# Attention value sums held in one PSUM bank for sixteen units

## The chip, the cores and the metric

One Trainium2 chip, one core of it. The metric is the device time of one execution, in microseconds, as the median of three runs. The engines are TensorE (PE, with its weight loads, PEld), VectorE (DVE), ScalarE (ACT), GpSimd (POOL) and SyncE (SP), which issues the transfers.

## The reference

Two mixers of 2048 rows of 512 are computed and blended by a gate. Branch A is a Fourier transform over the hidden and the sequence axis, as products with cosine and sine matrices; branch B is attention with 32 heads of 16.

```python
a = jnp.einsum("bsd,ed->bse", x, dft_hid_re)
b = jnp.einsum("bsd,ed->bse", x, dft_hid_im)
y = jnp.einsum("ts,bse->bte", dft_seq_re, a) - jnp.einsum("ts,bse->bte", dft_seq_im, b)
...
scores = jnp.einsum("bhqd,bhkd->bhqk", q, k) * scale
p = _softmax(scores, axis=-1)
o = jnp.einsum("bhqk,bhkd->bhqd", p, v)
...
g = _sigmoid((x * gate_w).sum(-1, keepdims=True))
return g * a + (1 - g) * b
```

## The kernel before

All products run on TensorE. The heads are worked in 16 pairs. For each pair the scores are made twice: once as tiles of 128 queries by 512 keys, of which VectorE takes the row maxima (line 260), and once transposed, 128 keys by 512 queries with the maximum already subtracted in the product, of which ScalarE takes the exponential into the SBUF tile `pt` (line 798). A **unit** `u` is one block of 128 keys against 1024 queries of one half `hf`, for both heads of the pair: four exponential tiles, two blocks of 512 queries (`qb`) for each of two heads (`h`). Sixteen units make one half of a pair; there are 512 units.

The **value sum** of a unit is four matmuls of 32 columns each (line 833), one for each query block and head, that fill one PSUM bank together. `pv(us)` takes two units into a bank (`start` on the first, `stop` on the second); then ScalarE copies the bank into `oe` (line 842), and GpSimd adds `oe` onto the SBUF tile `osum` (line 848). For the first two units of a half ScalarE copies straight into `osum` (line 839). After the sixteenth unit SP stores `osum` to memory (line 851). The last sixteen units go through `pv_last`, which holds a bank for eight units and is another code path.

The order of the work is written out by hand as patterns (lines 940 to 943), one **run** to a pattern. Each letter is a slot: `a` a tile for a maximum (line 258), `s` a score tile for an exponential (line 797), and beside a slot stands one matmul `d` of the Fourier chain or of the output projection (line 473). Those use 64 rows of the array each, so a slot's tile and its `d` run side by side on the two halves of the array. The bar at the end of a pattern calls `values()`, which takes the sum of two units.

```python
    FULL = "a s a s a s a s s a s a s a a s |"
    THIN = "aS s a s a s s a s a s a a sA |"
    EVEN = "aA s s a s ^ s d s sA a d sS |", "a s a sS a ^ s a s s s s a |"
    TEN = "aA s s a s ^ s s s a a sS |", "a s a sS a ^ s s s s s aA |"
```

`pairs()` issues 24 runs of THIN, 192 of FULL and 32 of EVEN and TEN; eight more runs of the last sixteen units end the kernel.

PSUM has eight banks here. One (`psD`) is kept for the Fourier chain, seven circulate: `bank()` hands out the one that the planner's estimate `free[]` says comes back first, and `read_by` estimates when its reader is done. What is handed out is fixed when the program is built; on the chip a matmul into a bank waits for the semaphore of the reader before. `pt` has four buffers.

Of the kernel before, what the change touches and what calls it, by code (L numbers as in the profile page):

```python
# [10 lines left out]
F32 = mybir.dt.float32  # L11
F32R = mybir.dt.float32r
AF = mybir.ActivationFunctionType
ALU = mybir.AluOpType
AX = mybir.AxisListType

P = 128
S = 2048
D = 512
H = 32  # L20
DH = 16
NP = H // 2
KT = D // P
NT = S // P
UNITS = NP * 32
# [7 lines left out]
def mix_kernel(ctx: ExitStack, tc: tile.TileContext, xa_t, xa, wqkv, w_hid, w_seq, wo, gate_w, out):  # L33
# [5 lines left out]
    nc = tc.nc  # L39
# [11 lines left out]
    o_d = [dram.tile([NP, 64, S // 2], F32, name=f"o{hf}") for hf in range(2)]  # L51
# [27 lines left out]
    def turn_of(kind):  # L79

        group = {"f": banks, "s": banks[:4], "a": [*banks[4:], psD], "r": [banks[6], banks[4]]}[kind]
        turns[kind] += 1
        pool = group[(turns[kind] - 1) % len(group)]
        return pool.tile([P, 512], F32, name="d" if pool is psD else "t")
# [47 lines left out]
    with tc.tile_pool(name="qk", bufs=1, reuse_waits="tile") as pool:  # L132
# [27 lines left out]
        ps = turn_of("f")  # L160
# [3 lines left out]
        x, raw = xab[0][:, :, :, :P], first[0].rearrange("p (s t) -> p s t", s=4)  # L164
        nc.scalar.copy(x[:, :, 0], raw)
        for ct in range(4):
            cols = slice(ct * P, (ct + 1) * P)
# [14 lines left out]
        for tb in range(4):  # L182
# [4 lines left out]
            for c in range(2):  # L187
                if tb == 0 and c == 0:
                    pss = [turn_of("f") for _ in range(4)]
                    for kt, w, v in [(kt, w, v) for kt in range(2) for w, v in ((wh, 0), (wl, 0), (wh, 1))]:  # L190
                        for ct in range(4):
                            nc.tensor.matmul(pss[ct], w[:, c, kt, ct * P:(ct + 1) * P],  # L192
                                             xab[tb][:, :, v, kt * P:(kt + 1) * P],
                                             start=kt == 0 and w is wh and not v, stop=False)
# [7 lines left out]
                for ct in range(4):  # L202
                    ps = turn_of("f")
# [13 lines left out]
    vt = main.tile([P, NT, NP, 33], F32, name="vt")  # L217
# [156 lines left out]
    for s in range(4):  # L374
        ps = turn_of("s")
# [21 lines left out]
    work = ctx.enter_context(tc.tile_pool(name="work", bufs=1, side="right", reuse_waits="tile"))  # L397
# [28 lines left out]
    now, free, dve, act = 0.0, [0.0] * 7, 0.0, 0.0  # L426

    def bank(i=None):

        nonlocal now  # L430
        if i is None:
            i = min(range(7), key=lambda j: free[j])
        now = max(now, free[i] + 0.7)
        return i, banks[i].tile([P, 512], F32, name="t")

    def read_by(i, kind):

        nonlocal dve, act
        if kind == "a":
            dve = max(now + 2.0, dve) + 2.6  # L440
            free[i] = dve + 0.4
        else:
            act = max(now + 2.0, act) + 2.1
            free[i] = act + 0.5
# [209 lines left out]
    few, by_others = [], set()  # L654

    def finish(ps, t, y, other=False, n=1):
        if other:

            for c in range(n):
                cols = slice(c * D // n, (c + 1) * D // n)  # L660
                tmp = few[0][:, t % 4, cols]
                nc.scalar.activation(tmp, ps[:, cols], AF.Copy, scale=omg[:, t:t + 1])
                nc.gpsimd.tensor_tensor(y[:, cols], y[:, cols], tmp, ALU.add)
            return
        nc.vector.scalar_tensor_tensor(y, ps, omg[:, t:t + 1], y, op0=ALU.mult, op1=ALU.add)  # L665
# [100 lines left out]
    last_pairs = []  # L766

    def last_pair(fill):
        few.append(work.tile([P, 4, D], F32, name="few", tag="pt", bufs=4))
        x = last_pairs[1]  # L770
        x.copy(4)
        by_others.add(6)
        pump(fill, 3)
        x.turn()
        pump(fill, 3)
        x.back()
        drain(fill)
        x.products((0,))


    pts = {}

    def scores(u, qb, h, ps=None):
        p, r = divmod(u, 32)
        hf, kt = divmod(r, 16)
        q0 = hf * 1024 + qb * 512
        if u >= UNITS - 16:

            blk, kt = divmod(kt, 8)
            q0, kt = 1024 + blk * 512, 2 * kt + qb  # L790
        if u not in pts:
            pts[u] = work.tile([P, 4, 512], F32, name="pt", bufs=4)
        if ps is None:
            i, ps = bank()
            read_by(i, "s")
        rr = slice(64 * h, 64 * h + 64)
        nc.tensor.matmul(ps, ks[p % 2][rr, kt * P:(kt + 1) * P], qs[p % 2][rr, q0:q0 + 512], start=True, stop=True)  # L797
        return nc.scalar.activation(pts[u][:, 2 * qb + h], ps, AF.Exp, bias=0.0, scale=DH ** -0.5)  # L798

    held = []  # L800

    def pv_last(u):
        nonlocal now
        blk, k2 = divmod(u - UNITS + 16, 8)
        pt = pts.pop(u)
        if k2 == 0:
            i, acc = bank()
            free[i] = 1e9
            held[:] = [i]
            last_pairs.append(LastPair(blk, acc))  # L810
        acc = last_pairs[-1].acc
        for j in range(4):
            x, h = divmod(j, 2)
            nc.tensor.matmul(acc[32 * j:32 * j + 32], vt[:, 2 * k2 + x, NP - 1, h:h + 32], pt[:, j],  # L814
                             start=k2 == 0, stop=k2 == 7)
        now += 3.75
        if blk == 0 and k2 == 7:
            last_pairs[0].copy(1)
            free[held[0]] = now + 6

    osum = work.tile([P, 2, 512], F32, name="osum", tag="w15")

    def pv(us):

        nonlocal now
        i, acc = bank()
        for u in us:
            p, r = divmod(u, 32)
            hf, kt = divmod(r, 16)
            pt = pts.pop(u)  # L830
            for j in range(4):
                h = j % 2
                nc.tensor.matmul(acc[32 * j:32 * j + 32], vt[:, kt, p, h:h + 32], pt[:, j],  # L833
                                 start=u == us[0], stop=u == us[-1])
        now += 3.75 * len(us) + 1
        read_by(i, "s")
        o = osum[:, hf]
        if kt + 1 == len(us):
            nc.scalar.copy(o, acc)
            return  # L840
        oe = work.tile([P, 512], F32, name="oe", bufs=2)
        nc.scalar.copy(oe, acc)  # L842
        adds.append(partial(add_sum, o, oe, p, hf, kt == NT - 1))

    adds = []

    def add_sum(o, oe, p, hf, whole):
        nc.gpsimd.tensor_tensor(o, o, oe, ALU.add)  # L848
        if whole:
            for qb in range(2):  # L850
                nc.sync.dma_start(o_d[hf][p, :, qb * 512:(qb + 1) * 512], o[64 * qb:64 * qb + 64])

    def add_sums():
        while adds:
            adds.pop(0)()

    def take(gen, n, whole=True):

# [23 lines left out]
    def pump(gen, n):  # L882
        for x in take(gen, n, False):
            issue(x, None)
# [11 lines left out]
    for p in range(2, NP):  # L896
        u = 32 * (p - 1)
        at(u - 18, load_q, p, LOW)
        for kb in range(4):
            cols = slice(kb * 512, (kb + 1) * 512)  # L900
# [7 lines left out]
    for hf in range(2):  # L908
        for ct in range(4):
            n = 3 if hf and ct == 3 else 4  # L910
# [43 lines left out]
    users, valued = [], 0  # L954
# [8 lines left out]
            else:  # L963
                users.append((kind, scores(*x)))

    def values():
        nonlocal valued
        us = valued, valued + 1
        valued += 2
        if us[0] < UNITS - 16:  # L970
            pv(us)
        else:
            for u in us:
                pv_last(u)

    def segment(pattern, half, ds, stop, between=None, hold=True):


        nonlocal now
        nonlocal users  # L980
        before, users = users, []
        ds, late = iter(ds), []
        back = late if hold else None
        for n, slot in enumerate(pattern.split()):
            if slot == "|":
                for f in late:
                    f()
                add_sums()
                run_plan(valued)
                if between:  # L990
                    between()
                values()
                continue
            if slot == "^":
                if deferred:
                    deferred.pop(0)()
                continue
            now += 1
            ahead = n and len(slot) == 1 and slot != "d" and pattern in (THIN, *TEN)
            if ahead:  # L1000
                score(slot[0], 1 - half)
            if len(slot) == 1:
                x = next(ds, None)
                if x:

                    before = before if x[0].begun else None
                    i = issue(x, half, stop, back)
                    users = []
                    if before:
                        tc.add_manual_dep(  # L1010
                            i.ins, dict(before[::-1]).get("s", before[0][1]).ins.name,
                            mybir.DependencyInfo(mybir.DependencyClass.Sync, mybir.DependencyReason.DATA))
                        before = None
            if not ahead and slot != "d":
                score(slot[0], 1 - half)
            if len(slot) == 2:
                score(slot[1].lower(), half)
        if deferred:
            deferred.pop(0)()
# [46 lines left out]
    for hf, qts in ((1, range(2)), (1, range(2, 5)), (1, range(5, 8)), (0, range(2))):  # L1066
        for half in range(2):
            ds = take(proj(hf, (3,), [held_bank] * (len(qts) - 1) + one, qts, half == 1), 9, False)
            pattern = "s s ^ s s s s s s |" if len(qts) < 3 else "s s ^ s s d s s s s |"
            if valued == UNITS - 2:  # L1070
                pattern = "s s s s d d |"
# [39 lines left out]
```

## Time and profile before

| | |
|---|---|
| median of three runs | 1651.18 us (1650.62 to 1653.74) |
| span of the profiled execution | 1649.2 us |
| TensorE busy, matmuls | 1641.4 us |
| VectorE busy | 1356.8 us |
| ScalarE busy | 1268.2 us |
| GpSimd busy | 754.5 us |
| copies into `oe` (line 842) | 217, 588 ns each, 127.5 us |
| additions onto `osum` (line 848) | 217, 1289 ns each, 279.7 us |

The profile is of one execution; its span of 1649.2 us lies 2.0 us below the median. Matmul records of TensorE are pipelined and their ends modelled, so its busy share does not tell how close it is to its best; the steps from one matmul to the next do. A row of a group has line, engine, operation, output and inputs, sizes and count, then busy time and the mean length of one in ns, and last the idle time of the engine before it and what ended it. Each value matmul of the program is two records in the trace.

### The profile page before, as it was taken

What the parts mean: (1) busy time and instruction counts of PE and PEld (TensorE: products, weight loads), DVE (VectorE), ACT (ScalarE), POOL (GpSimd) and SP (SyncE); (2) the same over time, 40 slices, a digit from 0 to 9 for tenths busy, and PEclk for the clock granted to TensorE, in tenths of its full rate; (3) what the DMA queues carried; (4) which work ended last, traced back from release to release, by engine and by line L of the source; (5) the groups of instructions that cost most, each with busy time, mean ns of one, the idle gap of its engine ahead of it and who ended that gap; (6) DMA issues with size and microseconds to landing.
All of it is one profiled execution on the core that took longest, in us unless ns stands there. A gap on an engine that the chain in (4) does not pass through costs nothing.

```text
span 1649.2 us, 35245 instructions
## 1 busy us (share of the span) xinstructions
PE 1641.4 (100%) x13169; PEld 1017.0 (62%) x13169; DVE 1356.8 (82%) x2285; ACT 1268.2 (77%) x2487; POOL 754.5 (46%) x813
## 2 busy tenths in 40 slices
PE   9999999999999999999999999999999999999998
PEld 7888855556656666566665666666666556655544
DVE  5469988888888888888888888888888888877776
ACT  5312188888888888888888888887888888899996
POOL 0224643554544555545454565554545566332341
PEclk9999999999999999999999999999999999999999
DMA  9953301112221224222227334322222233451024
GB/s 291 353 161 135 155 14 38 29 53 66 67 72 52 62 86 134 74 62 70 57 75 258 86 94 116 96 77 68 66 72 74 81 111 107 156 195 45 15 53 143
DMA packets 93346, 165.67 MB, mean 100 GB/s; under 512 B 23456, under 2 KB 26408, under 8 KB 92024
## 3 DMA queue, kind: packets, MB, share of 16 engines
q1 hardware_dynamic: 88536, 162.64, 31.9%
q8 instruction: 104, 1.70, 0.4%
q0 software_dynamic: 4352, 0.39, 0.2%
q14 instruction: 66, 0.54, 0.1%
q10 hardware_dynamic: 288, 0.39, 0.1%
HBM read 107.73 MB, written 54.52 MB: 98 GB/s over the span
## 4 chain that ended last, share of the span: by engine, by line
PE 99%; DMA 0%; DVE 0%; ACT 0%; DVEq 0%; SPq 0%; issue 0%
PE d L473 46%; PE t L833 28%; PE t L258 6%; PE t L797 6%; PE t L354 5%; PE t L92 2%; PE t L91 2%; PE t L93 2%; PE t L814 1%; PE t L473 1%; PE t L378 1%; PE t L192 0%; DMA raw<-wqkv 0%; DVE yp L665 0%; PE t L751 0%; PE t L729 0%
## 5 line engine op out<-in xcount | busy, mean ns | idle before, releaser
L260 DVE TENSOR_REDUCE mx<-t 128x1 f32<-128x512 f32 x2008 | 1232.8, 684 | 223.1 <-PE t L258 205.4
L798 ACT ACTIVATE pt<-t 128x512 f32<-128x512 f32 x2048 | 1031.1, 626 | 14.9 <-PE t L797 3.2
L258 PE MATMUL t<-ks,qs 64*128 64x512 f32 x2008 | 748.4, 406 | 0.0
L797 PE MATMUL t<-qs,ks 64*128 64x512 f32 x2048 | 729.4, 394 | 0.2
L473 PE MATMUL d<-xab,ch 64*128 64x512 f32 x2016 | 644.6, 394 | 0.0
L833 PE MATMUL t<-pt,vt 128*32 128x512 f32 x3968 | 477.1, 598 | 0.0
L473 PEld LDWEIGHTS d<-xab,ch 64*128 64x128 f32 x2016 | 366.7, 184 | 168.6 <-issue 67.1
L473 PE MATMUL d<-xab,cl 64*128 64x512 f32 x1008 | 397.7, 395 | 0.0
L258 PEld LDWEIGHTS t<-ks,qs 64*128 64x128 f32 x2008 | 355.9, 184 | 50.4 <-ACT pt L798 24.5
L797 PEld LDWEIGHTS t<-qs,ks 64*128 64x128 f32 x2048 | 368.5, 184 | 28.2 <-DVE mx L260 7.4
L848 POOL TENSOR_TENSOR osum<-osum,oe 128x512 f32<-128x512 f32 x217 | 279.7, 1289 | 157.4 <-ACT oe L842 155.3
L842 ACT COPY oe<-t 128x512 f32<-128x512 f32 x217 | 127.5, 588 | 182.3 <-PE t L833 175.2
L473 PEld LDWEIGHTS d<-xab,cl 64*128 64x128 f32 x1008 | 185.6, 184 | 85.8 <-issue 41.9
L833 PEld LDWEIGHTS t<-pt,vt 128*32 128x32 f32 x3968 | 103.6, 109 | 217.8 <-issue 149.1
L418 POOL CAST ch<-craw 128x512 fp32r<-128x512 f32 x126 | 77.4, 614 | 339.7 <-PE t L258 227.4
L419 POOL TENSOR_TENSOR cl<-craw,ch 128x512 fp32r<-128x512 f32 x126 | 162.5, 1289 | 10.2
L281 POOL DMA_DIRECT2D qs<-mt x132 | 73.8, 565 | 80.9 <-DVE mt L277 71.3
L473 PE MATMUL d<-wo_hl,o_hl 64*128 64x512 f32 x288 | 77.8, 402 | 0.0
L473 PE MATMUL d<-wre,xab 64*128 64x512 f32 x288 | 72.2, 394 | 0.0
L473 PEld LDWEIGHTS d<-wo_hl,o_hl 64*128 64x128 f32 x288 | 49.5, 184 | 15.9 <-ACT pt L798 13.4
L473 PEld LDWEIGHTS d<-wre,xab 64*128 64x128 f32 x288 | 50.9, 184 | 0.9
L91 PE MATMUL t<-xab,wh 128*128 128x512 f32 x120 | 46.7, 389 | 0.0
(123 smaller groups left out, 938.8 us busy)
## 6 DMA issues: line engine op xcount, KB each, us to landing
craw<-w_seq SPq DMA_DIRECT2D x128, 256.0 KB
qk<-hl SPq DMA_DIRECT2D x32, 512.0 KB
qs<-qk SPq DMA_DIRECT2D x84, 128.0 KB
ks<-qk SPq DMA_DIRECT2D x288, 32.0 KB
b<-hl SPq DMA_DIRECT2D x16, 512.0 KB
xab<-b SPq DMA_DIRECT2D x16, 512.0 KB
o<-osum SPq DMA_DIRECT2D x62, 128.0 KB
oh<-nh SPq DMA_DIRECT2D x12, 512.0 KB
```

Of the source, the lines that this page charges most:

```text
L91: nc.tensor.matmul(ps, sh, mh, start=first, stop=False)
L258: nc.tensor.matmul(ps, qs[p % 2][r, qt * P:(qt + 1) * P], ks[p % 2][r, kb * 512:(kb + 1) * 512], start=True, stop=True)
L260: user = nc.vector.tensor_reduce(mx[p % 2][:, h, qt, kb:kb + 1], ps, AX.X, ALU.max)
L354: i = nc.tensor.matmul(ps[c], st[r], mv[r], start=phase < 2 and j == 0, stop=phase > 1 and j == 11)
L418: nc.gpsimd.tensor_copy(h1, raw)
L419: nc.gpsimd.tensor_tensor(l1, raw, h1.bitcast(F32), ALU.subtract)
L473: i = nc.tensor.matmul(self.ps, st[r], mv[r], start=not self.begun, stop=stop)
L797: nc.tensor.matmul(ps, ks[p % 2][rr, kt * P:(kt + 1) * P], qs[p % 2][rr, q0:q0 + 512], start=True, stop=True)
L798: return nc.scalar.activation(pts[u][:, 2 * qb + h], ps, AF.Exp, bias=0.0, scale=DH ** -0.5)
L833: nc.tensor.matmul(acc[32 * j:32 * j + 32], vt[:, kt, p, h:h + 32], pt[:, j], start=u == us[0], stop=u == us[-1])
L842: nc.scalar.copy(oe, acc)
L848: nc.gpsimd.tensor_tensor(o, o, oe, ALU.add)
```

## The change

- `pv` takes one unit instead of a list. At the first unit of a half it claims a bank and holds it (`free = 1e9`, no tile can get it); the other fifteen units add into the same bank. After the sixteenth ScalarE copies it into `osum`, and SP's stores follow at the next bar. The copies into `oe` and the additions on GpSimd are gone.
- The exponentials' buffers are split by head: `pt` is now a tile of half the size for each unit and head, eight buffers instead of four. `few`, which uses the same buffers at the very end, is halved likewise.
- `values` takes the number of units as an argument; its default, and the only value used, is two, as before.

```diff
-        if u not in pts:
-            pts[u] = work.tile([P, 4, 512], F32, name="pt", bufs=4)
+        if (u, h) not in pts:
+            pts[u, h] = work.tile([P, 2, 512], F32, name="pt", bufs=8)
...
-        return nc.scalar.activation(pts[u][:, 2 * qb + h], ps, AF.Exp, bias=0.0, scale=DH ** -0.5)
+        return nc.scalar.activation(pts[u, h][:, qb], ps, AF.Exp, bias=0.0, scale=DH ** -0.5)
...
-    def pv(us):
+    accs = []
+
+    def pv(u):
 
         nonlocal now
-        i, acc = bank()
-        for u in us:
-            p, r = divmod(u, 32)
-            hf, kt = divmod(r, 16)
-            pt = pts.pop(u)
-            for j in range(4):
-                h = j % 2
-                nc.tensor.matmul(acc[32 * j:32 * j + 32], vt[:, kt, p, h:h + 32], pt[:, j],
-                                 start=u == us[0], stop=u == us[-1])
-        now += 3.75 * len(us) + 1
-        read_by(i, "s")
-        o = osum[:, hf]
-        if kt + 1 == len(us):
-            nc.scalar.copy(o, acc)
-            return
-        oe = work.tile([P, 512], F32, name="oe", bufs=2)
-        nc.scalar.copy(oe, acc)
-        adds.append(partial(add_sum, o, oe, p, hf, kt == NT - 1))
-
-    adds = []
-
-    def add_sum(o, oe, p, hf, whole):
-        nc.gpsimd.tensor_tensor(o, o, oe, ALU.add)
-        if whole:
-            for qb in range(2):
-                nc.sync.dma_start(o_d[hf][p, :, qb * 512:(qb + 1) * 512], o[64 * qb:64 * qb + 64])
...
+        p, r = divmod(u, 32)
+        hf, kt = divmod(r, 16)
+        if kt == 0:
+            accs[:] = bank()
+            free[accs[0]] = 1e9
+        i, acc = accs
+        pt = [pts.pop((u, h)) for h in range(2)]
+        for j in range(4):
+            x, h = divmod(j, 2)
+            nc.tensor.matmul(acc[32 * j:32 * j + 32], vt[:, kt, p, h:h + 32], pt[h][:, x], start=kt == 0, stop=kt == NT - 1)
+        now += 3.75
+        if kt == NT - 1:
+            read_by(i, "s")
+            nc.scalar.copy(osum[:, hf], acc)
+            stores.append(partial(store_sum, p, hf))
+
+    stores = []
+
+    def store_sum(p, hf):
+        for qb in range(2):
+            nc.sync.dma_start(o_d[hf][p, :, qb * 512:(qb + 1) * 512], osum[64 * qb:64 * qb + 64, hf])
```

The kinds of instructions and their sequence on TensorE, VectorE and SP are the same in both programs; ScalarE loses 217 copies and GpSimd 217 additions. What moves on TensorE are the waits. Here are the last four slots of a FULL run and the value sum, before. The `t` with a number is a PSUM tile, `d` the Fourier chain's bank; in brackets stands the engine whose semaphore the row waits for.

```order
L797 MATMUL t_11175<-qs0_938,ks0_939 128x512 [waits DVE_49]
L473 MATMUL d_10715<-xab3_180,ch_10841 128x512
L258 MATMUL t_11179<-ks1_941,qs1_940 128x512 [waits Activation_49]
L473 MATMUL d_10715<-xab3_180,ch_10841 128x512
L258 MATMUL t_11183<-ks1_941,qs1_940 128x512 [waits DVE_49]
L473 MATMUL d_10715<-xab3_180,cl_10842 128x512
L797 MATMUL t_11187<-qs0_938,ks0_939 128x512 [waits Activation_49]
L833 MATMUL t_11200<-pt_11073,vt_942 32x512 [waits DVE_49]
L833 MATMUL t_11200<-pt_11073,vt_942 32x512 x3
L833 MATMUL t_11200<-pt_11090,vt_942 32x512 x4
```

The same slots of the same run, now:

```order
L797 MATMUL t_11027<-qs0_938,ks0_939 128x512 [waits Activation_49]
L473 MATMUL d_10572<-xab3_180,ch_10700 128x512
L258 MATMUL t_11031<-ks1_941,qs1_940 128x512 [waits DVE_49]
L473 MATMUL d_10572<-xab3_180,ch_10700 128x512
L258 MATMUL t_11035<-ks1_941,qs1_940 128x512 [waits Activation_49]
L473 MATMUL d_10572<-xab3_180,cl_10701 128x512
L797 MATMUL t_11039<-qs0_938,ks0_939 128x512 [waits DVE_49]
L837 MATMUL t_10643<-pt_10973,vt_942 32x512
L837 MATMUL t_10643<-pt_10927,vt_942 32x512
```

Each wait stands one slot earlier: slots 13 to 16 waited for VectorE, ScalarE, VectorE, ScalarE in turn, and the value sum for VectorE; now slots 13 to 16 wait for ScalarE, VectorE, ScalarE, VectorE, and the value sum waits for no bank. Its tile, `t_10643`, is an old one, claimed at the half's first unit.

The other place is a run of TEN, its last three slots and the value sum, before:

```order
L797 MATMUL t_21582<-qs1_940,ks1_941 128x512 [waits Activation_49]
L473 MATMUL d_21488<-wo_hl_20823,o_hl2_21126 128x512
L258 MATMUL t_21586<-ks0_939,qs0_938 128x512 [waits Activation_49]
L258 MATMUL t_21589<-ks0_939,qs0_938 128x512 [waits DVE_49]
L833 MATMUL t_21597<-pt_21506,vt_942 32x512 [waits Activation_49]
```

And now:

```order
L797 MATMUL t_21254<-qs1_940,ks1_941 128x512 [waits Activation_49]
L473 MATMUL d_21161<-wo_hl_20511,o_hl2_20805 128x512
L258 MATMUL t_21258<-ks0_939,qs0_938 128x512 [waits DVE_49]
L258 MATMUL t_21261<-ks0_939,qs0_938 128x512 [waits Activation_49]
L837 MATMUL t_20954<-pt_21201,vt_942 32x512
```

The wait for ScalarE that stood at the value sum stands at the last tile of the run.

More of the change, by code (lines that the diff above doesn't have):

```diff
@@ L660, in finish @@
                 cols = slice(c * D // n, (c + 1) * D // n)
-                tmp = few[0][:, t % 4, cols]
+                tmp = few[0][:, t % 4 // 2, cols]
                 nc.scalar.activation(tmp, ps[:, cols], AF.Copy, scale=omg[:, t:t + 1])
@@ L768, in last_pair @@
     def last_pair(fill):
-        few.append(work.tile([P, 4, D], F32, name="few", tag="pt", bufs=4))
+        few.append(work.tile([P, 2, D], F32, name="few", tag="pt", bufs=8))
         x = last_pairs[1]
@@ L813, in pv_last @@
             x, h = divmod(j, 2)
-            nc.tensor.matmul(acc[32 * j:32 * j + 32], vt[:, 2 * k2 + x, NP - 1, h:h + 32], pt[:, j],
+            nc.tensor.matmul(acc[32 * j:32 * j + 32], vt[:, 2 * k2 + x, NP - 1, h:h + 32], pt[h][:, x],
                              start=k2 == 0, stop=k2 == 7)
@@ L821, in mix_kernel @@
     osum = work.tile([P, 2, 512], F32, name="osum", tag="w15")
-    def pv(us):
+    accs = []
+    def pv(u):
         nonlocal now
-        i, acc = bank()
-        for u in us:
-            p, r = divmod(u, 32)
-            hf, kt = divmod(r, 16)
-            pt = pts.pop(u)
-            for j in range(4):
-                h = j % 2
-                nc.tensor.matmul(acc[32 * j:32 * j + 32], vt[:, kt, p, h:h + 32], pt[:, j],
-                                 start=u == us[0], stop=u == us[-1])
-        now += 3.75 * len(us) + 1
-        read_by(i, "s")
-        o = osum[:, hf]
-        if kt + 1 == len(us):
-            nc.scalar.copy(o, acc)
-            return
-        oe = work.tile([P, 512], F32, name="oe", bufs=2)
-        nc.scalar.copy(oe, acc)
-        adds.append(partial(add_sum, o, oe, p, hf, kt == NT - 1))
-    adds = []
-    def add_sum(o, oe, p, hf, whole):
-        nc.gpsimd.tensor_tensor(o, o, oe, ALU.add)
-        if whole:
-            for qb in range(2):
-                nc.sync.dma_start(o_d[hf][p, :, qb * 512:(qb + 1) * 512], o[64 * qb:64 * qb + 64])
-    def add_sums():
-        while adds:
-            adds.pop(0)()
+        p, r = divmod(u, 32)
[4 more added lines that the diff above has]
+        i, acc = accs
+        pt = [pts.pop((u, h)) for h in range(2)]
+        for j in range(4):
[10 more added lines that the diff above has]
+            nc.sync.dma_start(o_d[hf][p, :, qb * 512:(qb + 1) * 512], osum[64 * qb:64 * qb + 64, hf])
     def take(gen, n, whole=True):
@@ L964, in score, with values, segment @@
                 users.append((kind, scores(*x)))
[L966 to L976, printed above, removed]
+    def values(n):
+        nonlocal valued, now
+        for u in range(valued, valued + n):
+            (pv if u < UNITS - 16 else pv_last)(u)
+        valued += n
+        now += 1
+    def segment(pattern, half, ds, stop, between=None, hold=True, n_values=2):
         nonlocal now
@@ L987, in segment @@
                     f()
-                add_sums()
+                while stores:
+                    stores.pop(0)()
                 run_plan(valued)
@@ L991, in segment @@
                     between()
-                values()
+                values(n_values)
                 continue
```

## The prediction

> **What bounds the kernel now.** I read the page first: span, engines, clock, groups.
>
> ```profile
> span 1649.2 us, 35245 instructions
> PE 1641.4 (100%) x13169; PEld 1017.0 (62%) x13169; DVE 1356.8 (82%) x2285; ACT 1268.2 (77%) x2487; POOL 754.5 (46%) x813
> PE 99%; DMA 0%; DVE 0%; ACT 0%; DVEq 0%; SPq 0%; issue 0%
> L260 DVE TENSOR_REDUCE mx<-t 128x1 f32<-128x512 f32 x2008 | 1232.8, 684 | 223.1 <-PE t L258 205.4
> L798 ACT ACTIVATE pt<-t 128x512 f32<-128x512 f32 x2048 | 1031.1, 626 | 14.9 <-PE t L797 3.2
> L833 PE MATMUL t<-pt,vt 128*32 128x512 f32 x3968 | 477.1, 598 | 0.0
> L848 POOL TENSOR_TENSOR osum<-osum,oe 128x512 f32<-128x512 f32 x217 | 279.7, 1289 | 157.4 <-ACT oe L842 155.3
> L842 ACT COPY oe<-t 128x512 f32<-128x512 f32 x217 | 127.5, 588 | 182.3 <-PE t L833 175.2
> ```
>
> TensorE is the chain: 99% of the span is followed back through it. A busy TensorE can still be stepping slower than it could, so I looked for slots that slip. The waits name who held TensorE's weight loads in front of the value sums, and the chain of waits gives the beat of the long middle stage.
>
> ```profile
> PEld t L833 <- DVE mx L260: 60.5, 213, 0.3
> 360.76 1.86 PE t L833 x16
> 1347.22 1.86 PE t L833 x16
> ```
>
> From 360.76 to 1347.22 us lie 986.46 us, 172 runs of 5.735 us each (172 is the whole number that fits the single run below, 5.74 us). The 60.5 us are waits of weight loads, not lost matmul time. What a run costs shows only slot by slot, so I took the timeline of one run of the FULL pattern, from the end of one value sum to the next. In each row: start, length, engine, line.
>
> ```profile
> 505.86 0.50 PE L473 MATMUL d<-xab,cl 64*128 64x512 f32 x1
> 505.87 0.50 PE L258 MATMUL t<-ks,qs 64*128 64x512 f32 x1
> 506.06 0.59 ACT L842 COPY oe<-t 128x512 f32<-128x512 f32 x1 [1.10 <-PE t L833]
> 506.20 0.39 PE L797 MATMUL t<-qs,ks 64*128 64x512 f32 x1
> 506.41 3.68 DVE L260 TENSOR_REDUCE mx<-t 128x1 f32<-128x512 f32 x6 [0.86 <-PE t L258]
> 506.66 3.53 ACT L798 ACTIVATE pt<-t 128x512 f32<-128x512 f32 x7
> 509.17 0.39 PE L473 MATMUL d<-xab,ch 64*128 64x512 f32 x1
> 509.18 0.18 PEld L473 LDWEIGHTS d<-xab,cl 64*128 64x128 f32 x1
> 509.27 0.18 PEld L797 LDWEIGHTS t<-qs,ks 64*128 64x128 f32 x1
> 509.40 0.39 PE L473 MATMUL d<-xab,cl 64*128 64x512 f32 x1
> 509.43 0.39 PE L797 MATMUL t<-qs,ks 64*128 64x512 f32 x1
> 509.75 0.16 PEld L833 LDWEIGHTS t<-pt,vt 128*32 128x32 f32 x8 [0.30 <-DVE mx L260]
> ```
>
> The reader is to see three things. First, slots step by 0.23 us (509.17 to 509.40), while the maxima step by (3.68 - 0.684) / 5 = 0.599 us and the exponentials by (3.53 - 0.626) / 6 = 0.484 us. Sixteen tiles are filled in some 3.6 us and drained more slowly, so unread tiles pile up towards the run's end: PSUM banks are what TensorE runs short of. Second, the release of a bank: the fifth exponential ends at 506.66 + 4 x 0.484 + 0.626 = 509.22 us, and the weights that waited for its bank load at 509.27, 0.05 us later. Third, that load came 0.09 us behind its neighbour (509.18) and the pair still started 0.23 us after the one before: a load has slack. After the value sum there is none, because the load (505.86) can't run ahead; there the next pair comes after 0.34 us instead of 0.23, so a fully exposed load costs 0.11 us. Between the last slot (509.43) and the value sum's load (509.75) stand 0.32 us.
>
> **The change, part by part.** *Copies and additions.* It removes 217 ScalarE copies (127.5 us) and 217 GpSimd additions (279.7 us). Neither engine is on the chain. For ScalarE I asked whether the copy delays the exponentials: the copy begins at 506.06 and the next operation could follow 0.48 us later, at 506.54, but the first score's matmul starts only at 506.20, and the first maximum began 0.54 us after its own matmul (505.87 to 506.41). So in this stage the exponential starts at about 506.66 anyway and the gain is at most some hundredths: I take nothing. The 31 copies of whole sums stay, in other places. GpSimd's other work has idle time around it; nothing there.
>
> *The held bank.* Seven banks circulate (the eighth carries the Fourier chain). Before, a run makes 17 claims on them, 16 tiles and then the value sum. After, it makes 16 claims on six. Claim k on n banks needs release k - n of the run's tiles (before, the old sum's bank comes back in time for slot 7, its copy ending at 506.65). So before, slot 16 needs the ninth release and the value sum the tenth; after, slot 16 itself needs the tenth. In this run the releases end, maxima at 506.41 + 0.684 + 0.599 (j - 1), exponentials at 506.66 + 0.626 + 0.484 (i - 1): the ninth is the fifth exponential, 509.22; the tenth is the fifth maximum, 506.41 + 0.684 + 4 x 0.599 = 509.49 us. The order of the built program agrees: each wait moves up by one slot, and the value sum loses its own.
>
> Before, the wait for the tenth release (509.49 + 0.05 = 509.54) stood at a load that could not go before 509.75 anyway: it cost nothing. After, it stands at slot 16, whose load went at 509.18 to 509.27. The load goes at 509.54, exposed, the matmul starts 0.11 us later at 509.65 and the value sum's load 0.32 us after that, at 509.97 instead of 509.75: **0.22 us more per run**. Behind slot 16's load everything of TensorE is queued in order, so the Fourier products wait too, and no engine makes it good: VectorE, done with its eighth maximum at 506.41 + 7 x 0.599 + 0.684 = 511.29, is idle before each run as it is. There are 192 such runs (96 pairs): 42.2 us.
>
> THIN, 24 runs, and EVEN and TEN, 32 runs, have other rows. First THIN, then TEN:
>
> ```profile
> 266.97 0.50 PE L258 MATMUL t<-ks,qs 64*128 64x512 f32 x1
> 267.51 3.68 DVE L260 TENSOR_REDUCE mx<-t 128x1 f32<-128x512 f32 x6 [0.65 <-PE t L258]
> 267.65 4.03 ACT L798 ACTIVATE pt<-t 128x512 f32<-128x512 f32 x8
> 270.26 0.18 PEld L258 LDWEIGHTS t<-ks,qs 64*128 64x128 f32 x1
> 270.68 0.16 PEld L833 LDWEIGHTS t<-pt,vt 128*32 128x32 f32 x8 [0.24 <-DVE mx L260]
> ```
>
> ```profile
> 1499.21 0.49 PE L473 MATMUL d<-wo_hl,o_hl 64*128 64x512 f32 x1
> 1499.97 2.56 ACT L798 ACTIVATE pt<-t 128x512 f32<-128x512 f32 x5
> 1501.60 0.30 PEld L258 LDWEIGHTS t<-ks,qs 64*128 64x128 f32 x2 [0.19 <-ACT pt L798]
> 1502.14 0.16 PEld L833 LDWEIGHTS t<-pt,vt 128*32 128x32 f32 x8 [0.24 <-ACT pt L798]
> ```
>
> In THIN the last slot of the changed order waits for ScalarE: by the planner's rotation for the sixth exponential, which ends at 267.65 + 5 x 0.486 + 0.626 = 270.71 (0.486 = (4.03 - 0.626) / 7). With 0.05, 0.11 and 0.32 the value sum comes at 271.19 instead of 270.68, 0.51 us later. Here the copy did delay the exponentials: without it they can start 0.54 us after the first matmul, at 267.51, and then it is 0.37. I take the middle, 0.44: 24 x 0.44 = 10.6 us. In TEN a run has 13 tiles; the last needs release 13 - 6 = 7, the fourth exponential, at 1499.97 + 3 x 0.484 + 0.626 = 1502.05. The value sum moves to 1502.05 + 0.05 + 0.11 + 0.32 = 1502.53 instead of 1502.14: 0.39 us, 32 runs, 12.5 us.
>
> *The exponentials' buffers.* Eight halves by head in place of four wholes hold the same bytes. A half is freed no later than the whole was, and in the group above the exponentials stood idle 14.9 us in all: nothing, and at best a part of those 14.9 us on an engine off the chain. The row buffers of the very end are cut the same way, with no operation more or less.
>
> *Stores of finished sums.* SP issues the same 62, at the same place in its queue, now behind ScalarE's copy instead of GpSimd's addition, a run after it was issued; the copy is done 0.8 us into that run (506.06 + 0.59 against 505.86). Nothing.
>
> The sum is 42.2 + 10.6 + 12.5 = 65.3 us on an execution whose span is 1649.2 us. The median of three runs, 1651.18, lies 2.0 us above the span, and I carry that: 1651.2 + 65.3 = 1716 us.
>
> The bounds. Below: if a late load were not exposed (its 0.11 us hidden), the three terms are 0.11, 0.33 and 0.28 us, 21.1 + 7.9 + 9.0 = 38 us, 1689. Above: other slots are moved to later releases too; slot 15 now waits for the fifth exponential and starts at 509.22 + 0.05 + 0.11 = 509.38, so that slot 16 can't start before 509.61, only 0.04 us under its own bound. If one more exposed load per run were not absorbed, 248 x 0.11 = 27 us come on top, 1743.
>
> A rule of the Trainium skill speaks against this change: "Perfetto Trace Analysis", section "Matmul Optimizations", asks that all eight PSUM banks be in use so that instructions can overlap. It gives no price; by it the sum would be some loss, by the rows it is 65 us.
>
> **The rivals.** *No change.* The waits of weight loads in the first rows, 60.5 us, cost nothing before, so moved by one slot they might still cost nothing: 1651 us. For it speaks the slack of 0.09 us that was seen to be absorbed. Against it: the load of slot 16 moves by 0.27 us beyond 509.27. It decides at a tenth release before about 509.30, which would need a fifth maximum 0.2 us earlier.
>
> *Faster.* ScalarE's copy was what held the banks: without it the exponentials start up to 0.48 us earlier, the sixth exponential (509.71 now) overtakes the fifth maximum, and six banks serve better than seven did. The point is an exponential that can start at or before 506.41. Then the waits that still slow the runs go. From the first slot to the value sum's load FULL takes 3.89 us and needs 0.34 + 14 x 0.23 + 0.32 = 3.88; THIN's 14 pairs take 3.71 and need 3.42; TEN's 11 pairs take 2.93 and need 2.73: 192 x 0.01 + 24 x 0.29 + 32 x 0.20 = 15 us, 1636 us. Against it: in FULL the first score starts at 506.20 whatever ScalarE does, and the bank that slot 16 waits for is fixed in the program, VectorE's.
>
> *The clock falls.* The stalls recur in every run, and the granted clock could answer.
>
> ```profile
> 337.30:1444.00 1106.70, 1106.70 (x9260) 673.98 (x9260) 949.55 (x1600) 914.13 (x1783) 567.06 (x608) 1.00 0.31 89
> ```
>
> The granted clock (1.00, third from the end) held through the middle stage, with a step of 0.32 us at each run's end. If a tenth of these 1107 us ran at half the clock, 111 us would come on top: 1827 us. The Trainium skill, "TensorE: Matmul & The Clock Gate", section "A second HAM failure mode: psum-queue depth-cycling", tells of a kernel whose short idles between groups at each bank cycle made the clock swing between half and full. The 1.00 here does not bear it out so far.
>
> *The change doesn't do what it says*: the planner, which counts bank times in its own units, might spread tiles so that a seventh bank is free after all. The order shows one value tile for sixteen units and the shifted waits, so this is hardly open; it would give the time of no change.
>
> **How the numbers follow.** The forecast, slower by 38 to 92 us, has 0.85. No change by hidden waits has 0.04, faster 0.05, the clock 0.02; slower by less than 38 us has 0.04. Runs of this kernel differ by 0.2% (1650.62 to 1653.74), so 0.2% is what a measurement can tell from none. Slower by more than that: 0.85 + 0.02 + 0.04 = 0.91; the same 0.04; faster 0.05. The range is the forecast's own, 1689 to 1743, with 0.15 left out.
>
> **What would show it.** In the changed profile: TensorE still 99% of the chain; runs in the middle of about 5.96 us instead of 5.735; the waits of the value sum's load on VectorE gone and waits of the lines 258 and 797 on VectorE and ScalarE grown; the last slot's load 0.05 us behind the end of a fifth maximum; VectorE's idle time before its first maximum longer; ScalarE some 67% and GpSimd some 28% busy, (1268.2 - 127.5) and (754.5 - 279.7) of 1716. I am wrong if the runs keep 5.73 us, or if they lengthen while the last slot's load is not the late one.

## The result and the profile after

The changed kernel takes 1709.84 us (median of four runs, 1709.82 to 1710.13) against 1650.9 us; the ratio is 1.0356, 95% interval 1.0342 to 1.0371. It is slower by 59 us; 1716 had been forecast, between 1689 and 1743. The page after, with the lines that answer to those of before:

```profile
span 1708.4 us, 34633 instructions
PE 1699.6 (99%) x13169; PEld 1028.4 (60%) x13169; DVE 1356.1 (79%) x2285; ACT 1143.9 (67%) x2270; POOL 479.5 (28%) x596
PE 99%; ACT 0%; DMA 0%; DVE 0%; DVEq 0%; SPq 0%; issue 0%
L260 DVE TENSOR_REDUCE mx<-t 128x1 f32<-128x512 f32 x2008 | 1232.0, 681 | 282.2 <-PE t L258 255.2
L798 ACT ACTIVATE pt<-t 128x512 f32<-128x512 f32 x2048 | 1031.6, 620 | 381.7 <-PE t L797 319.1
L837 PE MATMUL t<-pt,vt 128*32 128x512 f32 x3968 | 477.1, 598 | 0.0
```

TensorE has the same 13169 matmuls and is still 99% of the chain; the value sums' busy time is the same 477.1 us to the tenth. VectorE and ScalarE have the same work on the tiles and sit idle longer before it, waiting for TensorE. (Of ScalarE's 381.7 us, 182.3 us stood before the copies in the old kernel, so the rise in this row is not all new.) GpSimd's 279.7 us of additions and ScalarE's 127.5 us of copies are gone and have bought next to nothing. "PE 99%" reads like before; only the steps show that TensorE is being held.

Where the time went, from the starts of the 248 value sums in the two traces. An interval runs from the start of one value sum to the start of the next and is counted with the run inside it; the first THIN run lies before the first value sum. The columns are the sums of the stages in us, the mean length of a half's first seven intervals, and that of the eighth, from a half's last value sum to the next half's first:

| stage | before | after | difference | first seven before, after | eighth before, after |
|---|---|---|---|---|---|
| up to the first value sum | 215.2 | 215.0 | -0.1 | | |
| THIN, 23 intervals | 128.2 | 136.0 | +7.8 | 5.57, 5.95 | 5.57, 5.58 |
| FULL, 192 intervals | 1101.3 | 1141.5 | +40.2 | 5.735, 5.973 | 5.74, 5.75 |
| EVEN and TEN, 32 intervals | 153.4 | 163.8 | +10.4 | 4.79, 5.17 | 4.78, 4.78 |
| from the last one's start to the end | 51.2 | 52.0 | +0.8 | | |

The loss lies in the three stages with a held bank, and inside them in seven intervals of eight. A half's eighth interval kept its time to about 0.01 us. Here is one held FULL run of the changed kernel, from its first slot's load to the value sum's load, and the next value sum (start, length, engine, line):

```profile
661.97 0.18 PEld L473 LDWEIGHTS d<-xab,cl 64*128 64x128 f32 x1 [0.84 <-ACT nh L87]
662.51 4.27 DVE L260 TENSOR_REDUCE mx<-t 128x1 f32<-128x512 f32 x7 [1.11 <-PE t L258]
662.77 4.03 ACT L798 ACTIVATE pt<-t 128x512 f32<-128x512 f32 x8 [1.41 <-PE t L797]
665.38 0.18 PEld L258 LDWEIGHTS t<-ks,qs 64*128 64x128 f32 x1
665.64 0.18 PEld L797 LDWEIGHTS t<-qs,ks 64*128 64x128 f32 x1
665.72 0.43 PE L797 MATMUL t<-qs,ks 64*128 64x512 f32 x1
666.08 0.16 PEld L837 LDWEIGHTS t<-pt,vt 128*32 128x32 f32 x8 [0.25 <-issue]
672.07 0.16 PEld L837 LDWEIGHTS t<-pt,vt 128*32 128x32 f32 x8 [0.28 <-issue]
```

Maxima step by (4.27 - 0.681) / 6 = 0.598 us, so the fifth ends at 662.51 + 4 x 0.598 + 0.681 = 665.58 us. The last slot's load goes at 665.64, 0.06 behind it, its matmul at 665.72 and the value sum's load at 666.08, 0.44 us after the slot's load. Over the 168 held FULL runs of the trace the mean is 0.11 us from that load to its matmul and 0.33 from there to the value sum. From one value sum to the next it is 5.99 us. The release before it says the same: exponentials step by (4.03 - 0.620) / 7 = 0.487, the fifth ends at 662.77 + 4 x 0.487 + 0.620 = 665.34, and slot 15's load goes at 665.38. The single run is no exception. In all 168 held FULL runs the last slot's load goes 0.05 to 0.06 us behind the end of the fifth maximum, where before it went 0.05 to 0.25 us ahead of it. In the 21 held THIN runs it goes 0.05 us behind the sixth exponential, and in the 27 held runs of TEN 0.05 us behind the fourth: the releases that the prediction named for them.

Now the eighth interval, from the end of a half to the first value sum of the next:

```profile
636.43 1.92 PE L837 MATMUL t<-pt,vt 128*32 128x512 f32 x16
638.42 0.58 ACT L841 COPY osum<-t 128x512 f32<-128x512 f32 x1 [0.17 <-PE t L837]
641.70 0.18 PEld L797 LDWEIGHTS t<-qs,ks 64*128 64x128 f32 x1
642.18 0.16 PEld L837 LDWEIGHTS t<-pt,vt 128*32 128x32 f32 x8 [0.30 <-DVE mx L260]
```

The copy at 638.42 gives the held bank back, the next is claimed only by the value sum at 642.18, and between them seven banks circulate: 5.75 us. In that one run the value sum waits for VectorE again, as every run did before. The waits count them:

```profile
  DVE mx L260: 7.2, 24
  ACT pt L798: 2.0, 7
```

24 times on VectorE instead of 213, and 7 on ScalarE instead of 32: together 31, as many as there are halves, and so as many as there are claims of a bank by a value sum.

### The profile page after: what moved, and what is told of

Its sections match the earlier page's. It is cut to its first block, busy times and chain, and to the rows that moved or that the text cites. A ratio compares the mean times of both kernels' runs of the same rounds, so it can differ in the third digit from the quotient of the medians.

```text
span 1708.4 us, 34633 instructions
## 1 busy us (share of the span) xinstructions
PE 1699.6 (99%) x13169; PEld 1028.4 (60%) x13169; DVE 1356.1 (79%) x2285; ACT 1143.9 (67%) x2270; POOL 479.5 (28%) x596
## 4 chain that ended last, share of the span: by engine, by line
PE 99%; ACT 0%; DMA 0%; DVE 0%; DVEq 0%; SPq 0%; issue 0%
PE d L473 33%; PE t L837 27%; PE t L797 14%; PE t L258 12%; PE t L354 5%; PE t L93 2%; PE t L92 2%; PE t L91 2%; PE t L814 1%; PE t L378 1%; PE t L473 1%; PE t L192 0%; ACT pt L798 0%; DMA raw<-wqkv 0%; PE t L751 0%; PE t L729 0%
## 5 line engine op out<-in xcount | busy, mean ns | idle before, releaser
L798 ACT ACTIVATE pt<-t 128x512 f32<-128x512 f32 x2048 | 1031.6, 620 | 381.7 <-PE t L797 319.1
L797 PE MATMUL t<-qs,ks 64*128 64x512 f32 x2048 | 767.7, 411 | 0.1
L258 PE MATMUL t<-ks,qs 64*128 64x512 f32 x2008 | 761.9, 411 | 0.0
L837 PE MATMUL t<-pt,vt 128*32 128x512 f32 x3968 | 477.1, 598 | 0.0
L473 PE MATMUL d<-wo_hl,o_hl 64*128 64x512 f32 x288 | 84.9, 421 | 0.0
L473 PE MATMUL d<-wre,xab 64*128 64x512 f32 x288 | 77.4, 411 | 0.0
L272 POOL CAST nhl<-nm 128x16 fp32r<-128x16 f32 (+1 forms) x33 | 6.5, 196 | 174.3 <-DVE nm L269 174.3
L473 PEld LDWEIGHTS d<-wre,xab 64*128 64x128 f32 x288 | 51.2, 184 | 0.4
L93 PE MATMUL t<-xab,wl 128*128 128x512 f32 x120 | 46.7, 389 | 0.0
```

The lines of the kernel that those rows point to most:

```text
L93: nc.tensor.matmul(ps, sl, mh, start=False, stop=last)
L258: nc.tensor.matmul(ps, qs[p % 2][r, qt * P:(qt + 1) * P], ks[p % 2][r, kb * 512:(kb + 1) * 512], start=True, stop=True)
L473: i = nc.tensor.matmul(self.ps, st[r], mv[r], start=not self.begun, stop=stop)
L798: return nc.scalar.activation(pts[u, h][:, qb], ps, AF.Exp, bias=0.0, scale=DH ** -0.5)
```

## The experiments

Seven kernels. The theory: slot k of a run on n free banks waits for release k - n of the run's tiles, and one bank fewer makes the last slot late. The rivals: the split of the buffers, the accumulation over sixteen units or its code path, and the removed work on ScalarE and GpSimd. All were timed in three rounds against the kernel before. It took 1653.84 us in the session of the first four and 1650.74 in that of the others, so ratios are to be preferred there.

**The split alone.** Two units to a bank with copies and additions as before, the buffers by head. Edit in the changed kernel, with `GROUP = 2` (the old copy and addition follow at the group's end):

```diff
-        if kt == 0:
+        if kt % GROUP == 0:
             accs[:] = bank()
...
-        if kt == NT - 1:
+        if kt % GROUP == GROUP - 1:
             read_by(i, "s")
```

Expected: 

> The old value sums (two units to a bank, copy and addition each run) with the exponentials' buffers split by head. If the missing seventh bank is the cause, as forecast: 1651 us, within 3 us, runs of the middle stage at 5.73 us. If the split of the buffers is the cause: near 1710 us. If each has a part: between.

Measured: 1656.23 us, ratio 1.0015 (1.0005 to 1.0025). That is 5 us above the 1651 expected and outside its 3; some 3 of the 5 are the session's, in which the kernel before took 1653.84. The split is not the cause of the 59 us, though not nothing either: some 2.4 us, by the interval 0.8 to 4.1, to which I come back below.

**The hold alone.** The changed kernel with the old whole buffers:

```diff
-        if (u, h) not in pts:
-            pts[u, h] = work.tile([P, 2, 512], F32, name="pt", bufs=8)
+        if u not in pts:
+            pts[u] = work.tile([P, 4, 512], F32, name="pt", bufs=4)
...
```

The reads and writes of `pt`, and `few`, follow suit.

Expected: 

> The held bank with the old whole exponential buffers (four, one for each unit). If the missing bank is the cause: 1710 us, within 3 us, seven of eight runs of the middle stage at 5.97 us. If the split of the buffers is the cause: 1651 us.

Measured: 1707.59 us, ratio 1.0325 (1.0309 to 1.034); the first seven intervals of a FULL half take 5.96 us, the eighth 5.75. The held bank carries the loss without the split.

**Six banks, nothing held.** The kernel before with one character changed:

```diff
-            i = min(range(7), key=lambda j: free[j])
+            i = min(range(6), key=lambda j: free[j])
```

Expected: 

> The kernel before, old value sums and all copies and additions, but with only six circulating banks instead of seven; the seventh is left unused after the first stage. If the number of banks is the cause: the last slot of every run, in all eight of eight, waits for the tenth release, 0.24 us in the middle stage and 0.38 in the others, 192 x 0.24 + 56 x 0.38 = 67 us, so 1718 us, between 1711 and 1730. If accumulating over sixteen units, or the held bank as such, is the cause: 1651 us.

Measured: 1726.99 us, ratio 1.0442 (1.0426 to 1.0457): 73 us slower, with no long accumulation, no held bank and no work removed. FULL takes 5.98 us in the first seven intervals and 5.99 in the eighth, so now all eight are long. Two value sums of it in a row:

```profile
600.51 1.85 PE t L833 x16
606.50 1.85 PE t L833 x16
```

The number of banks alone makes the step of 5.99 us. It came out 9 us above the sum of the expectation, inside its bounds. Against the trace of before, which is from a faster session and 76 us shorter, FULL is 47.9 us longer, THIN 10.6, EVEN and TEN 13.9, each 1.5 to 2 us more than its term; 3.8 us lie before the first and behind the last value sum, which the sum had left out. For TEN the reason shows: the value sum still claims a bank here, the fourteenth claim on six, and waits for the eighth release, the fifth exponential. In the trace of before that ends 3.32 us after the first slot; with 0.05 and the 1.85 of the value sum that makes 5.22, and the TEN intervals measure 5.23. In all 27 of these runs the value sum's load goes 0.05 us behind the fifth exponential.

**A bank held for four units, and for eight.** `GROUP = 4` and `GROUP = 8` in the edit of the first experiment.

Expected of four: 

> Buffers split, and a bank held for four units (two runs) instead of sixteen, with a copy and an addition every second run. If a run is long exactly when one bank is withdrawn during its slots: every second run long, half of 67 us, 1684 us, within 6 us. If the cause is the length of the accumulation, or the switch of code path, all runs alike, near 1710 or near 1651 us.

Expected of eight: 

> As the four-unit hold, but for eight units (four runs). If a run is long exactly when a bank is withdrawn during its slots: three of four runs long, 50 us, 1701 us, within 5 us. If something else in the held accumulation costs: the same as with sixteen units, 1710 us, or as with four.

Measured: 1687.25 us with four (ratio 1.0201, 1.0186 to 1.0216) and 1702.17 with eight (1.0311, 1.0294 to 1.0328). Value sums of the four-unit kernel in the middle stage:

```profile
630.35 1.92 PE L838 MATMUL t<-pt,vt 128*32 128x512 f32 x16
636.10 1.92 PE L838 MATMUL t<-pt,vt 128*32 128x512 f32 x16
642.09 1.92 PE L838 MATMUL t<-pt,vt 128*32 128x512 f32 x16
647.84 1.92 PE L838 MATMUL t<-pt,vt 128*32 128x512 f32 x16
653.81 1.92 PE L838 MATMUL t<-pt,vt 128*32 128x512 f32 x16
```

Steps of 5.75, 5.99, 5.75, 5.97 us: short when the bank is free, long when it is held, in turn. With eight units three are long and one short, 5.98, 5.97, 5.98, 5.74. A loss from the code path, or one that came with the long accumulation, could not alternate. One from an open accumulation as such could; that is ruled out by the six banks, where nothing is held and the step is the same.

**The removed work put back.** The changed kernel, with idle copies and additions in the old places:

```diff
+        if 2 < kt < NT - 1 and kt % 2:
+            oe = work.tile([P, 4, P], F32, name="oe", bufs=2)
+            i_cp = nc.scalar.copy(oe, zero.bitcast(F32).unsqueeze(1).broadcast_to([P, 4, P]))
...
+            stores.append(partial(nc.gpsimd.tensor_tensor, oe, oe, oe, ALU.add))
```

Expected: 

> The changed kernel with idle work put back: after each run's value sum but the first and last of a half, 186 in all, ScalarE copies a constant of the same size into the old buffer, waiting for the value sum as before, and GpSimd adds that buffer onto itself; the result does not use it. If the removed work was worth nothing outside the first pattern: 1710 us, and some 2 us more for the first pattern, where the copy delays the exponentials by 0.14 us. If the removed copies and additions gave a gain that the missing bank overlays: well above, 1720 us or more.

Measured: 1713.78 us, ratio 1.0381 (1.0366 to 1.0397). The THIN stage is 2.6 us longer than in the changed kernel (138.6 against 136.0), FULL 0.6, TEN none. So the removal was worth some 3 to 4 us, most of it in THIN, where the copy stands ahead of exponentials whose scores are ready, and next to nothing elsewhere. The stand-ins are not quite the old work: the copy takes 0.62 us for the old 0.59, the addition 1.04 for 1.29.

**One bank fewer still.** The changed kernel with `range(6)`:

```diff
-            i = min(range(7), key=lambda j: free[j])
+            i = min(range(6), key=lambda j: free[j])
```

Expected: 

> The changed kernel with one circulating bank fewer still: five while a sum is held, six in the first run of a half. If release k - n sets slot k: in the middle stage slot 16 waits for the eleventh release, the sixth exponential, 3.85 us after the first slot instead of 3.62, so 0.22 us on top of 5.97 in seven of eight runs and 0.24 in the eighth; in the last pattern the eighth release, the fifth exponential, 0.49 us more; in the first pattern about 0.5 us. 192 x 0.22 + 31 x 0.49 + 24 x 0.5 = 69 us on top of 1710, 1779 us, within 12 us. If the loss does not come from the number of banks: 1710 us.

Measured: 1804.38 us, ratio 1.093 (1.0914 to 1.0947), 25 us above the forecast of 1779 and outside its 12. FULL's first seven intervals take 6.35 us instead of 6.19, which puts FULL 27 us above its term; THIN stays 8 below its own, and 4 us lie before the first and behind the last value sum. A run:

```profile
844.31 4.96 DVE L260 TENSOR_REDUCE mx<-t 128x1 f32<-128x512 f32 x8 [1.39 <-PE t L258]
844.59 4.36 ACT L798 ACTIVATE pt<-t 128x512 f32<-128x512 f32 x8 [1.99 <-PE t L797]
845.65 0.18 PEld L797 LDWEIGHTS t<-qs,ks 64*128 64x128 f32 x1 [0.21 <-DVE mx L260]
846.25 0.18 PEld L258 LDWEIGHTS t<-ks,qs 64*128 64x128 f32 x1 [0.30 <-DVE mx L260]
846.85 0.18 PEld L258 LDWEIGHTS t<-ks,qs 64*128 64x128 f32 x1 [0.30 <-DVE mx L260]
847.81 0.18 PEld L797 LDWEIGHTS t<-qs,ks 64*128 64x128 f32 x1
848.24 0.16 PEld L837 LDWEIGHTS t<-pt,vt 128*32 128x32 f32 x8 [0.24 <-issue]
```

The eight exponentials take 4.36 us instead of 4.03. I had reckoned the releases at the pace of the readers, as if scores were always ready; on five banks TensorE is late so early (845.65) that ScalarE runs dry, and the release that slot 16 waits for comes later itself. In all 168 of these runs the last slot's load goes 0.05 us behind the sixth exponential, as forecast, but that one ends 4.02 us after the first slot instead of 3.85. The mechanism stood, and the size was off because it feeds back.

## Why the prediction was right

*What bounds, and the claims on the banks:* right. Every release that was computed has its load behind it: the fifth maximum in the held FULL runs, the fifth exponential one slot earlier, the sixth exponential in THIN, the fourth in TEN, each by 0.05 us. The price of a held FULL run, 0.22 us forecast, is 5.973 - 5.735 = 0.238.

*Which runs pay:* wrong in one step. "There are 192 such runs (96 pairs)" overlooked that the bank is free from the copy that ends a half to the first value sum of the next. One run in eight makes its 17 claims on seven banks, as every run did before, and keeps its time. For the same reason the value sum's waits for VectorE are not all gone, as had been forecast; 24 of 213 stay. The FULL stage measured 40.2 us for 42.2, because 168 runs at 0.238 and 24 at about 0.01 happen to come near 192 at 0.22: too many runs at too low a price, two errors that largely cancel. That much of the closeness is luck. In THIN and TEN they don't cancel: 7.8 us for 10.6 and 10.4 for 12.5. There the prices per held run were 0.37 for 0.44 and 0.37 for 0.39. The 0.44 was the middle between a delayed and an undelayed ScalarE, for which there was no ground, as the copy that delays it is gone in the changed kernel; the undelayed end, 0.37, was right. With 2.0, 2.8 and 2.1 us too much in the three stages and 0.7 too little at the two ends, that is the difference between 65.3 and 59 us.

*Copies and additions:* right. They were cover, not cost: ScalarE's busy time fell by 124 us and GpSimd's by 275 us, and the kernel slowed. Putting 186 pairs of them back costs 4 us.

*The exponentials' buffers:* wrong, by a small amount. Nothing was forecast, and the split costs about 2.4 us with seven banks (1656.23 against 1653.84) and about 2.3 with the held one (1709.84 against 1707.59). The last two times are from different sessions, but the traces agree: THIN, EVEN and TEN are the same in both kernels to 0.1 us, FULL is 2.6 us longer with the split. The next section but one has what is known of the reason.

*Stores, the end, the clock:* nearly as forecast. The part before the first value sum is the same to 0.1 us. From the start of the last value sum to the end of TensorE's last matmul it is 44.7 us before and 44.6 after, but from there to the end of the program 6.4 and then 7.4: the last landing of a transfer came 3.0 us after the last issue before, and comes 3.7 us after it now. The kernel with whole buffers has this longer end too, and the one with the split alone has not; why is open. The granted clock is 1.00 in the stretch that holds the middle stage:

```profile
346.00:1490.00 1144.00, 1144.00 (x9238) 686.52 (x9232) 945.38 (x1594) 812.34 (x1606) 353.14 (x437) 1.00 0.29 86
```

*The rivals.* That the waits stay hidden fell with the load at 665.64. That ScalarE's copy held the banks fell with the sixth experiment. The clock did not move: 0.24 us of stall in each 5.97 is not enough for it here.

No version of these beats the kernel before. The best that holds a bank over sixteen units keeps the whole buffers, at 1707.59 us; over four units it is 1687.25. By the count of claims, an eighth circulating bank would give the held runs their old step, and there is none to be had while the Fourier chain keeps its own; that was not tried.

## What to carry to other kernels

A bank that is held is paid for by the tiles that circulate on the others. Count the claims and the releases of one period, in order, and look which release the last claim waits for; a wait that moves from a place with slack to one with less costs the time by which it makes the next matmul late, and the weight load that can no longer run ahead is part of that. Work removed from engines that are off the chain is worth only what it let them start earlier, here 3 to 4 us, against the 59 that were lost on balance. The busy share says nothing here: the same 99% stood over runs of 5.735 and of 5.97 us.

## What was not expected of the hardware

A second wait on one instruction may not be free where the engine sits waiting. With buffers by head, each run can begin with a fresh buffer, and the exponential that first writes a fresh buffer often carries one more wait, which the program puts ahead of it as an instruction of its own on ScalarE's queue. The line of the exponentials, in the changed kernel and then with the whole buffers:

```profile
L798 ACTq EVENT_SEMAPHORE  x417: 17/17/17, 218.9 to 1690.3; - x139
```
```profile
L798 ACTq EVENT_SEMAPHORE  x241: 17/17/17, 218.9 to 1684.4; - x121
```

In the kernel before there are 274, with the split alone 376. In the changed kernel, then with whole buffers, a run's first score and its exponential:

```profile
656.33 0.39 PE L797 MATMUL t<-qs,ks 64*128 64x512 f32 x1
656.84 0.60 ACT L798 ACTIVATE pt<-t 128x512 f32<-128x512 f32 x1 [1.99 <-PE t L797]
```
```profile
655.66 0.39 PE L797 MATMUL t<-qs,ks 64*128 64x512 f32 x1
656.11 0.60 ACT L798 ACTIVATE pt<-t 128x512 f32<-128x512 f32 x1 [1.94 <-PE t L797]
```

0.51 us against 0.45. In every second FULL run the first exponential of the changed kernel starts 0.06 us later (0.86 us after the first slot against 0.80, means of the trace), and those are the runs of 5.98 us beside ones of 5.96. They are 96 of the 168 held runs, and the 96 alone have a semaphore instruction right ahead of their first exponential. Only 0.02 of the 0.06 us reaches the run's length: slot 15, which waits for an exponential, comes 0.04 us later, while the last slot's load, which waits for a maximum, goes at the same time in both. Each semaphore instruction lasts 17 ns. Between exponentials that follow each other no such delay shows, and they step by 0.48 us; at the head of a run, where ScalarE waits for TensorE, it does.

That this wait is the cause was read from the traces and the program, and not tried by itself. It does not explain the split's price with seven banks: there the same 96 first exponentials are late too (0.86 us against 0.80), yet the runs with and without the wait take the same 3.90 us from the first slot to the value sum, against 3.88 in the trace of the kernel before, which is from a faster session. What costs the 2.4 us there stays open.
